# Reciprocal denominators by way of DRAM, M laid out from SBUF to SBUF, and a new order around kv, gate and up

## The chip, the cores and the metric

The kernel runs on one core of one Trainium2 chip. The metric is the device time of one execution in microseconds, the median of three runs; before the change it is 115.38 us (114.64 to 117.84). One further execution was taken with the hardware profiler: it lasted 115.02 us, of which 113.3 us are the span of its instructions.

## The reference, cut to what matters

With S = 2048 tokens of width D = 640, H = 32 heads of 20, and bf16 tensors:

```python
xn = layernorm(x)                                   # (S, D), no scale or bias
q, k, v = split(xn @ wqkv)                          # heads of 20
pq, pk = phi(q), phi(k)                             # phi(t) = t + 1 if t > 0 else exp(t), + 1e-6
kv  = einsum("hsd,hse->hde", pk, v)                 # 20 x 20 for each head
z   = pk.sum(over s)
num = einsum("hqd,hde->hqe", pq, kv)
den = einsum("hqd,hd->hq", pq, z) + 1e-6
A   = (num / den) @ wo
r   = x @ w_r                                       # B works on the same normed x
idx = the 8 tokens with the largest r
y   = (silu(x[idx] @ w_gate) * (x[idx] @ w_up)) @ w_down * sigmoid(r[idx])
B   = x, with y added to the rows idx
out = A_x + A + B
```

The attention has no softmax, so kv and wo can be folded into one 640 x 640 matrix M; then A is (pq / den) @ M, where den differs by token and head.

## The kernel before, in words

TensorE (PE) multiplies, ScalarE (ACT) and VectorE (DVE) read the products from the eight PSUM banks, SyncE (SP) issues almost all transfers, GpSimd (POOL) does the two indirect ones. The order of each engine's instructions is the order in which the Python code calls the helpers: the schedule is written by hand. Each engine's queue is served in order, so an instruction that waits holds all that stand behind it; that holds for transfers issued from ACT too. A transfer signals on one of eight semaphores, used in turn: a new transfer waits until the transfer that had its semaphore before has landed.

Up to about 61 us the kernel loops over 16 token tiles of 128: layer norm, transposed tiles xnT, k, phi(k), the Gram matrix of phi(k) and xn in PSUM (`g_mm`), and the first six of twenty query blocks. A query block is 128 features (m = 0 to 4) by 512 tokens (b = 0 to 3): `q_mm` does five products of 128x512 (L345), `q_act` two activations on ACT (exp L352, relu L353, into buffers of which there are two of each), and `q_stt` joins them on DVE into `pqT` (L357).

Then comes the tail, which the change touches. It interleaves:

- the other fourteen query blocks, `q_next(bank)`;
- den: `den_mm(b, bank)` multiplies the queries of 512 tokens by a matrix of z (20 small products, L664); `den_act` takes Ln and Exp on ACT (L671, L672), which leaves 1/den as `rden`, 128 rows (4 groups of tokens x 32 heads) by 128 tokens;
- before the change `rep_mm` (4 products with a 0/1 matrix `sel4`, L676) and `rep_ev` (ACT copy, L680) spread `rden` to `rec`, where partition p holds the reciprocals of head p // 4 for the tokens along the row; `mult` (DVE, L684) multiplies 512 tokens of `pqT` by it;
- the expert: `moe_gu_mm` (40 products, L615), `moe_silu` (three activations L621 to L623), `moe_prod` and `moe_hm` (DVE, L626, L627, L630), `moe_ht` (transpose L634, copy L635), `moe_y` (48 products with `wd`, L641, then DVE L646 and an indirect add into the DRAM copy `xd` of xn, L647), and `reload`, five transfers (L654) that read `xd` back into `xn`;
- M: `kv_mm` (30 products, L690) and `kv_ev` (DVE, L699), then for six blocks j `m_mm` (two products, L707), `m_ev` (ACT L713, DVE L714) and `m_dma(j)`. Before the change `m_dma` wrote each block to DRAM (`md`, L718) and, behind the last, read all back in five strided transfers into `m_sb` (L722), which lies as row 5p + m at partition p, block m.

Last comes the out stage: for each of 16 token tiles t ten products of 128x320 (L812) into one of three bank pairs, ACT's copy (L840), DVE's two adds in `finish` (L802 adds the reloaded xn to x for tile t + 1, L808 adds that to the copy), and a store (L809). The last tile goes by DVE alone (L850, two halves). `finish` runs a few tiles behind the products.

## Time and profile before

| | us |
|---|---|
| median of three runs | 115.38 (114.64 to 117.84) |
| profiled execution: time | 115.02 |
| profiled execution: span | 113.3 |
| PE busy | 106.1 (94%) |
| DVE busy | 87.0 (77%) |
| ACT busy | 70.2 (62%) |
| granted TensorE clock | 0.999 |

All times within an execution are counted from the start of its span. In the groups, "busy, mean ns" is the time of a group and of one instruction; "idle before" is the time for which the engine had nothing to do ahead of them, with what ended it. PE's instructions overlap, so the spacing of its products in the timeline or the chain says more than the mean of one: ten products of the out stage, one tile, stand 1.36 us apart from the next ten. In a DMA row the last figure is the time from issue to landing.

### The profile page before, as it was taken

To read this page: it belongs to the slowest core of one execution; us is meant where nothing else is said; L and a number is where in the kernel's file an instruction comes from. 1 tells how busy PE (TensorE), PEld (TensorE's weight loads), DVE (VectorE), ACT (ScalarE), POOL (GpSimd) and SP (SyncE) were. 2 spreads that over 40 slices of the span, in tenths; PEclk is the share of its full clock that TensorE was granted. 3 is DMA by queue.
4 is the path that set the end of the run, shared out by engine and by line. 5 is a ranking of instruction groups with operands and counts; after the bars stand their busy time and mean duration, and the time that the engine had idled before them with its cause. 6 is when DMAs were issued, how large, how long until landed. Compare 5 with 4: busy or idle time off the path is not lost.

```text
span 113.3 us, 2428 instructions
## 1 busy us (share of the span) xinstructions
PE 106.1 (94%) x849; PEld 66.4 (59%) x849; DVE 87.0 (77%) x217; ACT 70.2 (62%) x170; POOL 24.6 (22%) x57
## 2 busy tenths in 40 slices
PE   5998999899999989999999999999896999999970
PEld 2365655556665655556676555766453777777740
DVE  0769988999999999972266977798759449999670
ACT  4149866666866645556637779859698087655530
POOL 3022222688866233330000040000410000000000
PEclk9999999999999999999999999999999999999999
DMA  2998244799996889999996564985458998624433
GB/s 82 369 365 284 59 114 119 191 241 260 222 291 188 179 191 257 255 287 369 343 384 213 119 120 75 378 298 168 116 122 245 287 366 291 232 94 144 174 116 116
DMA packets 29389, 24.71 MB, mean 218 GB/s; under 512 B 14353, under 2 KB 28097, under 8 KB 29377
## 3 DMA queue, kind: packets, MB, share of 16 engines
q1 hardware_dynamic: 28209, 23.45, 71.8%
q10 hardware_dynamic: 992, 1.07, 2.7%
q0 software_dynamic: 176, 0.05, 0.6%
q8 instruction: 6, 0.10, 0.4%
q14 instruction: 6, 0.05, 0.1%
HBM read 15.30 MB, written 6.14 MB: 189 GB/s over the span
## 4 chain that ended last, share of the span: by engine, by line
PE 76%; ACT 8%; DVE 8%; issue 4%; POOL 1%; DVEq 0%; ACTq 0%
PE ps L812 18%; PE ps L302 14%; PE ps L345 14%; PE ps L330 13%; PE ps L231 4%; ACT rq L353 4%; DVE pk L322 2%; PE ps L332 2%; ACT eq L352 2%; PE ps L337 2%; PE ps L707 2%; PE ps L615 2%; PE ps L690 2%; DVE xn L266 1%; PE ps L273 1%
## 5 line engine op out<-in xcount | busy, mean ns | idle before, releaser
L330 PE MATMUL ps<-xn,pk 128*128 128x512 bf16 x80 | 23.5, 382 | 0.7 <-DVE pk L322 0.7
L345 PE MATMUL ps<-xnT,wq 128*128 128x512 bf16 x100 | 23.9, 381 | 0.0
L812 PE MATMUL ps<-late,pqT 128*128 128x320 bf16 x160 | 22.4, 299 | 0.9 <-ACT rq L353 0.9
L302 PE MATMUL ps<-wk,xnT 128*128 128x321 bf16 (+1 forms) x140 | 21.4, 299 | 0.6 <-ACT rq L353 0.5
L812 PEld LDWEIGHTS <-pqT 128*128 128x128 bf16 x160 | 15.5, 98 | 7.2 <-issue 1.1
L313 ACT ACTIVATE ek<-ps 128x320 bf16<-128x320 f32 x28 | 12.3, 441 | 11.9 <-PE ps L302 11.9
L302 PEld LDWEIGHTS <-xnT 128*128 128x128 bf16 x140 | 13.5, 97 | 8.4 <-ACT xnT L279 0.6
L246 POOL TENSOR_TENSOR rs<-veps,pw 128x1 f32<-128x1 bf16 x15 | 12.8, 851 | 25.8 <-DVE veps L245 25.6
L322 DVE SCALAR_TENSOR_TENSOR pk<-ek,rk 128x640 bf16<-128x640 bf16 x16 | 13.1, 819 | 5.6 <-ACT rk L314 5.5
L352 ACT ACTIVATE eq<-ps 128x512 bf16<-128x512 f32 x20 | 12.2, 608 | 8.0 <-PE ps L345 6.7
L840 ACT CAST oall<-ps 128x640 bf16<-128x640 f32 x15 | 10.2, 694 | 9.9 <-PE ps L812 9.9
L357 DVE SCALAR_TENSOR_TENSOR pqT<-eq,rq 128x512 bf16<-128x512 bf16 x20 | 13.5, 687 | 3.5 <-ACT rq L353 3.4
L345 PEld LDWEIGHTS <-wq 128*128 128x128 bf16 x100 | 10.9, 118 | 8.5 <-issue 0.3
L330 PEld LDWEIGHTS <-pk 128*128 128x128 bf16 x80 | 8.4, 117 | 7.6 <-DVE pk L322 2.6
L314 ACT ACTIVATE rk<-ps 128x320 bf16<-128x320 f32 x28 | 12.2, 436 | 0.0
L353 ACT ACTIVATE rq<-ps 128x512 bf16<-128x512 f32 x20 | 12.1, 605 | 0.0
L332 PE MATMUL ps<-xn,pk 128*128 128x129 bf16 x48 | 10.6, 220 | 0.0
L238 DVE BATCH_NORM_STATS2 st<-x_sb 128x6 f32<-128x320 bf16 x16 | 7.8, 485 | 2.3 <-DMA x_sb<-in_A_x_dram 2.3
L808 DVE TENSOR_TENSOR oall<-oall,x_sb 128x640 bf16<-128x640 bf16 x15 | 7.3, 487 | 2.5 <-ACT oall L840 2.3
L802 DVE TENSOR_TENSOR x_sb<-x_sb,xn 128x640 bf16<-128x640 bf16 x16 | 7.7, 484 | 1.5 <-DMA xn<-xd 1.5
L240 DVE BATCH_NORM_STATS2 st<-x_sb 128x6 f32<-128x320 bf16 x16 | 7.6, 476 | 0.0
L266 DVE TENSOR_SCALAR xn<-cb,rs 128x640 bf16<-128x640 bf16 x15 | 6.3, 426 | 1.6 <-POOL rs L246 1.0
(137 smaller groups left out, 115.9 us busy)
## 6 DMA issues: line engine op xcount, KB each, us to landing
xd<-xn SPq DMA_DIRECT2D x16, 160.0 KB, 3.2
x_sb<-in_A_x_dram SPq DMA_DIRECT2D x6, 320.0 KB, 4.5
wg<-in_B_w_gate_dram SPq DMA_DIRECT2D x5, 384.0 KB, 3.8
wd<-in_B_w_down_dram SPq DMA_DIRECT2D x4, 480.0 KB, 6.1
xn<-xd SPq DMA_DIRECT2D x3, 640.0 KB, 10.1
out_dram<-oall SPq DMA_DIRECT2D x12, 160.0 KB, 1.8
wu<-in_B_w_up_dram SPq DMA_DIRECT2D x3, 384.0 KB, 4.3
wq<-in_A_wqkv_dram SPq DMA_DIRECT2D x1, 800.0 KB, 6.8
```

The costliest lines, as they stand in the source:

```text
L246: pool.tensor_tensor(out=rs[:, c], in0=veps[:, c], in1=pw[:, 0:1], op=ALU.pow)
L302: pe.matmul(ps[:, KB.get((t, h), h), 0:n], lhsT=(xcT if t < 2 else xnT)[:, kc, t * P : (t + 1) * P], rhs=wk[:, kc, h * HW : h * HW + n], s ...
L313: act.activation(e[:, s], ps[:, b, 0:HW], AF.Exp, scale=c)
L314: act.activation(r[:, s], ps[:, b, 0:HW], AF.Relu, scale=c)
L322: dve.scalar_tensor_tensor(out=pk[:, t, :], in0=e[:], scalar=1.0, in1=r[:], op0=ALU.min, op1=ALU.add)
L330: pe.matmul(bank(2 + m), lhsT=w, rhs=xn[:, t, 0:512], start=(t == 0), stop=(t == T - 1))
L332: pe.matmul(ps[:, 7, m * 129 : (m + 1) * 129], lhsT=w, rhs=xn[:, t, 512 : D + 1], start=(t == 0 and m == 0), stop=(t == T - 1), skip_group ...
L345: pe.matmul(bank(bk), lhsT=wq_m[:, kc, m, :], rhs=xnT[:, kc, b * TB : (b + 1) * TB], start=(kc == 0), stop=(kc == KC - 1))
L352: act.activation(e[:], bank(bk), AF.Exp)
L353: act.activation(r[:], bank(bk), AF.Relu)
L357: dve.scalar_tensor_tensor(out=pqT[:, m, b * TB : (b + 1) * TB], in0=e[:], scalar=1.0, in1=r[:], op0=ALU.min, op1=ALU.add)
L812: pe.matmul(ps[:, bk + b, 0:HW], lhsT=pqT[:, kc, t * P : (t + 1) * P], rhs=m_sb[:, kc, b * HW : (b + 1) * HW], start=(kc == 0), stop=(kc = ...
```

## The change

1. `rep_mm` and `rep_ev` go, and `sel4` with them. Instead `rep_out` stores `rden` to a DRAM tile `rd` (32 heads x 2048 tokens; one transfer for each 512 tokens, 128 rows of 256 bytes), and `rep_in` reads it back, each head's row four times, into `rec`. For b = 0 and 1 both are issued from SP, `rep_out` between the second and third of the four loads of `wd`, `rep_in` behind `m_dma(0)`. For b = 2 and b = 3 both are issued from ACT.
2. `m_dma` is one transfer for each block, from `mt` in SBUF to `m_sb` in SBUF. `md` and the five reads go.
3. `kv_mm` and `kv_ev` stand ahead of gate and up, and one query block more stands ahead of them.
4. Banks: M takes the pairs (2,7), (3,5), (4,0), gate and up (4,0), the last five query blocks 1, 0, 6, 7, 6. `den_mm(2, 7)` stands ahead of these five blocks instead of between the fourth and the fifth.
5. The first three tiles of the out stage are no longer interleaved over the row blocks of M; each tile takes its ten products in one go.

The same on ACT's queue, where the five last query blocks stand (`eq_3`, `rq_3` are the outputs of exp and relu for b = 3; `gl` is the tile in which `rec` lies). Before:

```order
L713 CAST late<-ps 40x320
L352 ACTIVATE eq_3_1291<-ps 128x512
L353 ACTIVATE rq_3_1292<-ps 128x512
L680 CAST gl<-ps 128x512
L352 ACTIVATE eq_3_1306<-ps 128x512
L353 ACTIVATE rq_3_1307<-ps 128x512
L680 CAST gl<-ps 128x512
L352 ACTIVATE eq_3_1322<-ps 128x512
```

Changed (helpers stand some lines higher: L345 is L339 now, L352 is L346, L812 is L800, L840 is L822):

```order
L707 CAST late<-ps 40x320
L665 ACTIVATE lden<-ps,eps_111 128x128
L666 ACTIVATE rden<-lden 128x128
L670 DMA rd<-rden 4x32x128
L346 ACTIVATE eq_3_1308<-ps 128x512
L347 ACTIVATE rq_3_1309<-ps 128x512
L346 ACTIVATE eq_3_1319<-ps 128x512
L347 ACTIVATE rq_3_1320<-ps 128x512
```

The two copies from PSUM are gone from between the query blocks; den's two activations and a DMA issue stand ahead of them.

ACT's queue from the last query block into the out stage, changed (`oall` is the copy of an out tile):

```order
L347 ACTIVATE rq_3_1356<-ps 128x512
L674 DMA gl<-rd 128x1x512
L822 CAST oall<-ps 128x640 x4
L665 ACTIVATE lden<-ps,eps_111 128x128
L666 ACTIVATE rden<-lden 128x128
L670 DMA rd<-rden 4x32x128
L822 CAST oall<-ps 128x640 x2
L674 DMA gl<-rd 128x1x512
L822 CAST oall<-ps 128x640 x6
```

For b = 3 the store stands behind the copy of tile 3 and the read behind that of tile 5; the copies of tile 6 and later stand behind the read.

SP's queue from the transposes of the Gram matrix (`gp`) to the reload of `xn`, before:

```order
L508 DMA_TRANSPOSE gp<-gt 128x5x128 x5
L128 DMA wd<-in_B_w_down_dram 128x3x640 x4
L718 DMA md<-late 120x640 x5
L718 DMA md<-late 40x640
L722 DMA late<-md 128x640 x5
L654 DMA xn<-xd 128x2x640 x2
L654 DMA xn<-xd 128x4x640 x3
```

Changed (`late` holds both `mt` and `m_sb`):

```order
L502 DMA_TRANSPOSE gp<-gt 128x5x128 x5
L129 DMA wd<-in_B_w_down_dram 128x3x640 x2
L670 DMA rd<-rden 4x32x128 x2
L129 DMA wd<-in_B_w_down_dram 128x3x640 x2
L712 DMA late<-late 24x5x640
L674 DMA gl<-rd 128x1x1024
L712 DMA late<-late 24x5x640 x4
L712 DMA late<-late 8x5x640
L648 DMA xn<-xd 128x2x640 x2
L648 DMA xn<-xd 128x4x640 x3
```

Two loads of `wd` now stand behind the stores of `rd`, and the five reads of M no longer stand ahead of the reload.

```diff
--- before.py
+++ after.py
@@ -105,7 +105,8 @@
     xd = tc.dram_tile([4 * S + P, QW], BF16, name="xd")
     xd_v = xd[0 : 4 * S, :].rearrange("(t p i) d -> p t i d", p=P, i=4)
     xd_row = xd[0 : 4 * S, :].rearrange("(n i) d -> n (i d)", i=4)
-    md = tc.dram_tile([D, D], BF16, name="md")
+    rd = tc.dram_tile([H, S], BF16, name="rd")
+    rd_v = rd[:].rearrange("h (b i n) -> i h b n", b=4, i=4)
 
     ctx.enter_context(tc.manual_schedule())
 
@@ -165,13 +166,6 @@
 
     def consts_a():
         g = {}
-        one = sb([P, 4, P], BF16, "sel4")
...
-        g["sel4"] = one
         hs = sb([P, H], BF16, "hsel")
@@ -671,13 +665,13 @@
         act.activation(lden[:, b0:b1, :], ps[:, bk, c : c + n].rearrange("p (b n) -> p b n", n=P), AF.Ln, bias=eps6[:])
         act.activation(rden[:, b0:b1, :], lden[:, b0:b1, :], AF.Exp, scale=-1.0)
 
-    def rep_mm(b, bk):
-        for i in range(4):
-            pe.matmul(ps[:, bk, i * P : (i + 1) * P], lhsT=cs["sel4"][:, i, :], rhs=rden[:, b, :],
-                      start=(i == 0), stop=True, skip_group_check=True)
-
-    def rep_ev(b, bk):
-        act.copy(rec[:, b * TB : (b + 1) * TB], bank(bk))
+    def rep_out(b0, b1, q=sp):
+        for b in range(b0, b1):
+            q.dma_start(rd_v[:, :, b, :], rden[:, b, :])
+
+    def rep_in(b0, b1, q=sp):
+        n = (b1 - b0) * TB
+        q.dma_start(rec[:, b0 * TB : b1 * TB], rd[:, b0 * TB : b1 * TB].unsqueeze(1).to_broadcast([H, 4, n]))
 
     def mult(o, n):
         sl = pqT[:, :, o : o + n]
@@ -701,29 +695,28 @@
             in0=ps[0:w, bk, c0 : c0 + w].rearrange("e (m p) -> e m p", m=KC),
             in1=mkf[0:w, :, 0:n], op=ALU.mult)
 
-    def m_mm(j, bk):
+    def m_mm(j, *bk):
         w = EB if j < 5 else 40
         for b in range(2):
-            pe.matmul(ps[0:w, bk + b, 0:HW], lhsT=kvT[0:w, j, 0:w], rhs=wo[0:w, j, b * HW : (b + 1) * HW],
+            pe.matmul(ps[0:w, bk[b], 0:HW], lhsT=kvT[0:w, j, 0:w], rhs=wo[0:w, j, b * HW : (b + 1) * HW],
                       start=True, stop=True)
 
-    def m_ev(j, bk):
+    def m_ev(j, *bk):
         w = EB if j < 5 else 40
         o = mt[0:w, j, :].rearrange("p (b f) -> p b f", b=2)
-        act.copy(o[:, 0, :], ps[0:w, bk, 0:HW])
-        dve.tensor_copy(o[:, 1, :], ps[0:w, bk + 1, 0:HW])
+        act.copy(o[:, 0, :], ps[0:w, bk[0], 0:HW])
+        dve.tensor_copy(o[:, 1, :], ps[0:w, bk[1], 0:HW])
 
     def m_dma(j):
-        w = EB if j < 5 else 40
-        sp.dma_start(md[j * EB : j * EB + w, :], mt[0:w, j, :])
-        if j == NJ - 1:
-            md_v = md[:].rearrange("(p m) d -> p m d", m=KC)
-            for m in range(KC):
-                sp.dma_start(m_sb[:, m, :], md_v[:, m, :])
+        n = 24 if j < 5 else 8
+        sp.dma_start(m_sb[24 * j : 24 * j + n, :, :], mt[0 : n * KC, j, :])
+
+    def ld_wd(k0):
+        ld_w(wd, B_w_down, k0, k0 + 3)
 
     gt_stage(moe_pick)
-    for k0 in range(0, FC, 3):
-        ld_w(wd, B_w_down, k0, k0 + 3)
+    ld_wd(0)
+    ld_wd(3)
     for bk in (2, 3, 4):
         q_fin(q_next(bk))
     q1 = q_next(5)
@@ -736,63 +729,58 @@
     q_act(*q1)
     q2 = q_next(2)
     moe_xt(6)
-    den_mm(1, 7)
     q_stt(*q1[0:2])
     q_act(*q2)
-    moe_gu_mm(3, 4)
+    den_mm(1, 7)
+    q1 = q_next(3)
     q_stt(*q2[0:2])
-    moe_silu(3, 4)
     den_act(0, 2, 7)
-    moe_prod(3, 4)
+    rep_out(0, 2)
+    ld_wd(6)
+    ld_wd(9)
+    q_act(*q1)
     for j in range(4):
         kv_mm(j, 6, j * EB)
     kv_mm(4, 5, 0)
     kv_mm(5, 5, EB)
-    q1 = q_next(0)
     for j in range(4):
         kv_ev(j, 6, j * EB)
     kv_ev(4, 5, 0)
     kv_ev(5, 5, EB)
-    q_act(*q1)
-    PAIR = (2, 4, 0)
+    moe_gu_mm(4, 0)
+    moe_silu(4, 0)
+    q_stt(*q1[0:2])
+    moe_prod(4, 0)
+    moe_hm()
+    MP = ((2, 7), (3, 5), (4, 0))
     for j in range(NJ):
-        m_mm(j, PAIR[j % 3])
-        m_ev(j, PAIR[j % 3])
+        m_mm(j, *MP[j % 3])
+        m_ev(j, *MP[j % 3])
         m_dma(j)
         if j == 0:
-            moe_hm()
+            rep_in(0, 2)
         if j == 1:
-            q2 = q_next(7)
+            q1 = q_next(1)
+            q_act(*q1)
+            moe_ht(6)
+        if j == 3:
             q_stt(*q1[0:2])
             moe_gate()
-            moe_ht(6)
-        if j == 2:
-            q_act(*q2)
-        if j == 3:
-            q_stt(*q2[0:2])
         if j == 4:
             moe_y(6)
-    q1 = q_next(7)
-    q_act(*q1)
-    rep_mm(0, 6)
-    rep_ev(0, 6)
-    q2 = q_next(0)
-    q_stt(*q1[0:2])
-    q_act(*q2)
-    rep_mm(1, 7)
-    q_stt(*q2[0:2])
+    den_mm(2, 7)
+    q1 = q_next(1)
+    den_act(2, 3, 7)
+    rep_out(2, 3, act)
+    q_fin(q1)
     mult(0, 512)
-    q1 = q_next(1)
-    rep_ev(1, 7)
-    q_fin(q1)
-    q1 = q_next(6)
-    q_fin(q1)
+    q_fin(q_next(0))
     reload()
-    den_mm(2, 7)
+    q_fin(q_next(6))
+    q_fin(q_next(7))
     mult(512, 512)
-    q1 = q_next(0)
-    den_act(2, 3, 7)
-    q_fin(q1)
+    q_fin(q_next(6))
+    rep_in(2, 3, act)
     assert qn[0] == len(Q_TAIL)
 
     evac = []
@@ -813,26 +801,20 @@
                   rhs=m_sb[:, kc, b * HW : (b + 1) * HW], start=(kc == 0), stop=(kc == KC - 1))
 
     OB = (2, 4, 0)
-    for kc in range(KC):
-        for t in range(3):
-            for b in range(2):
-                out_mm(t, OB[t], kc, b)
     for t in range(T):
         bk = OB[t % 3]
         if t == 3:
-            rep_mm(2, 6)
-            rep_ev(2, 6)
             den_mm(3, 7)
         if t == 4:
             den_act(3, 4, 7)
+            rep_out(3, 4, act)
             mult(1024, 512)
         if t == 6:
-            rep_mm(3, 6)
-            rep_ev(3, 6)
+            rep_in(3, 4, act)
         if t == 8:
             mult(1536, 512)
         last = t == T - 1
-        for i in range(2 * KC if t >= 3 else 0):
+        for i in range(2 * KC):
             kc, b = (i % KC, i // KC) if last else (i // 2, i % 2)
             out_mm(t, bk, kc, b)
         if not last:
```

5 lines of the change are left out of this document (removed).

## The prediction

> **What bounds the kernel now.** I read the page first, then who waits for PE and for whom PE waits, then the chain that ended last. From the page's first part:
>
> ```profile
> PE 106.1 (94%) x849; PEld 66.4 (59%) x849; DVE 87.0 (77%) x217; ACT 70.2 (62%) x170; POOL 24.6 (22%) x57
> ```
>
> PE works 94% of the span, so a gain must be work taken from PE or a wait of PE. The waits of PE over the whole span (in all, times, longest):
>
> ```profile
> PE ps L812 <- ACT rq L353: 0.9, 1, 0.9
> PE ps L330 <- DVE pk L322: 0.7, 2, 0.4
> PE ps L676 <- DVE late L646: 0.3, 1, 0.3
> ```
>
> The first and the third lie in the tail that is changed: the out stage waits 0.9 us for the activations of the last query block, which holds bank 0, and `rep_mm` waits 0.3 us for bank 6. Together 1.2 us. The chain of the end (start, length):
>
> ```profile
> 79.10 1.22 PE ps L345 x5
> ...
> 81.43 0.48 ACT gl L680
> ...
> 87.55 3.69 PE ps L812 x26
> 91.24 0.22 PE ps L676 x4
> 91.46 0.39 PE ps L664 x20
> ...
> 96.26 12.24 PE ps L812 x90
> 108.52 0.70 ACT oall L840
> ...
> 109.66 0.48 DVE oall L850
> ```
>
> From 80.3 to 87.55 ACT sets the pace (PE runs beside it, one block ahead); from 87.55 PE alone does, at 12.24/90 = 0.136 us a product, 1.36 us a tile; behind tile 14 come its copy, an add and the last tile's two adds.
>
> **What is removed.** `rep_mm`: four calls, 0.22 us each by the row of L676: 0.88 us of PE. The two waits above: 1.2 us. So 2.1 us is what PE can gain at most here. On ACT the two copies of 0.48 us (L680) leave the stretch that it paces. The 0/1 matrix `sel4` saves POOL some work near 22 us; the most it could give PE is the later of the L330 waits, 0.33 us of that 0.7; DVE waits for ACT between the two places, so I take 0, bounds 0 to 0.33.
>
> **Kv ahead of gate and up.** The chain of before in this stretch:
>
> ```profile
> 70.39 1.75 PE ps L615 x40
> 72.14 1.74 PE ps L690 x30
> 73.88 1.21 PE ps L345 x5
> 75.09 0.62 PE ps L707 x4
> 75.71 1.08 PE ps L345 x5
> 76.80 0.17 PE ps L634 x3
> ```
>
> ACT and DVE from the timeline (start, length):
>
> ```profile
> 70.31 0.64 ACT L353 ACTIVATE rq<-ps 128x512 bf16<-128x512 f32 x1
> 72.46 0.52 ACT L623 ACTIVATE gl<-sgl 128x384 bf16<-128x384 f32 x1
> 72.85 0.56 DVE L627 TENSOR_TENSOR gl<-ps,late 128x384 bf16<-128x384 f32 x1
> 73.42 1.95 DVE L699 TENSOR_TENSOR kvT<-ps,mk 120x120 bf16<-120x120 f32 x6
> 75.81 0.35 DVE L630 TENSOR_TENSOR late<-gl 128x384 bf16<-128x384 bf16 x1
> ```
>
> PE's pieces are the same, in the order query block, kv, gate and up, M, query block, `moe_ht`. From 70.39: 1.08 gives 71.47, kv 73.21, gate and up 74.96, M 75.58, query block 76.66. DVE starts `kv_ev` when four groups of kv are there, 71.47 + 4 x 0.29 = 72.6, say 72.7, and is done at 74.7; the join of the query block (0.6, in place of 0.56 for an operation of 384 columns) 75.3, gate's and up's two reads at 0.56 (L627 and its like) 76.45, L630 76.8. `moe_ht` on PE needs that: PE arrives at 76.66 and, with the signal's way, waits 0.2. ACT's three activations of silu, 0.52 each, run from 74.2 to 75.8, in time for L630. So this move costs 0.2 us; bounds 0 (DVE a little faster) and 0.5.
>
> SP waits here for `rden`: den's activations follow ACT's block at 70.95 and take about 0.9 (two of the width of L623), so `rep_out` issues at 71.9, and the two last loads of `wd`, which stood right behind the first two, come at about 72.8 and 73.3. `moe_y` needs the last quarter near 78.7 (it lies between 76.80 and 79.10 before). The transfers (KB, us from issue to landing; then L718, M's writes to DRAM, with the issue's length in ns and the landing, and the landing of L722, M's reads):
>
> ```profile
> wd<-in_B_w_down_dram SPq DMA_DIRECT2D x4, 480.0 KB, 6.1
> xd<-xn SPq DMA_DIRECT2D x16, 160.0 KB, 3.2
> out_dram<-oall SPq DMA_DIRECT2D x12, 160.0 KB, 1.8
> xn<-xd SPq DMA_DIRECT2D x2, 320.0 KB, 5.3
> L718 SPq DMA_DIRECT2D md<-late x6: 278/326/1134, 76.6 to 81.2; - x6
> DMA to landing us min/median/max: 2.0/2.8/2.9
> DMA to landing us min/median/max: 2.3/3.0/3.7
> ```
>
> The last load at 73.3 + 6.1 would be 79.4, 0.7 too late; but 6.1 holds four loads in a row behind transposes, and now half of the bytes are through when these two start. I take 0, bounds 0 and 0.7.
>
> **M.** One transfer a block, priced at L718's 2.8, at most 2.9: the last issues near 81, as before (81.2) and lands near 83.9; the out stage, which now needs all blocks for its first product, starts after 85. The five reads were not waited for either. Nothing; bounds 0 and 0.5. The reload stands behind five issues fewer and comes about 1 us earlier; that frees DVE earlier, not PE.
>
> **The five last query blocks.** `moe_ht` to the first of them took 2.3 us on PE (76.80 to 79.10); from 76.85 that is 79.15, and `den_mm(2)`, 0.39, ends at 79.55. ACT then has den's two activations and the store:
>
> ```profile
> 85.57 0.43 ACT L671 ACTIVATE lden<-ps,eps 128x128 f32<-128x128 f32 x1
> 86.03 0.31 ACT L672 ACTIVATE rden<-lden 128x128 bf16<-128x128 f32 x1
> 104.51 0.36 ACTq L809 DMA_DIRECT2D out_dram<-oall  x1
> ```
>
> 0.1 for the signal, 0.77 and 0.36 end at 80.8, when PE's first block (79.55 + 1.08 = 80.65) is there. Then 1.1 us a block: 81.9, 83.0, 84.1; the fourth waits for a buffer that DVE frees behind `mult(0)` and a join, about 84.9 to 86.0; the fifth 87.1. PE waits about 0.1 for bank 0 (DVE's last M half) at the second block, and 0.1 to 0.2 for bank 6 at the fifth (84.15 for 84.0); then it goes straight into tile 0, whose banks 2 and 3 are long free. New waits in all 0.2 + 0.2 = 0.4. If the issue held ACT for as much as 1.1 (the longest of L718), PE would lose 0.8 more; bounds 0 and 0.8.
>
> **The out stage.** Sum: 0.88 + 1.2 - 0.4 = 1.7 us earlier. Tile 14 ends at 108.5 - 1.7 = 106.8, tile 3 at 91.84, tile 5 at 94.56. ACT's copy of tile 3 (0.70) and den's activations (0.7, overlapping a little) end 1.36 later, 93.2; there `rep_out(3)` issues. ACT is through with tile 5 at 95.25 and then stands at `rep_in(3)` until the store has landed; PE feels that only when tile 9 needs a bank at 98.64. What depends on the landing of `rep_in(3)` is DVE:
>
> ```profile
> 97.77 1.48 DVE L684 TENSOR_TENSOR pqT<-pqT,gl 128x2560 bf16<-128x2560 bf16 x1
> 99.17 0.48 DVE L802 TENSOR_TENSOR x_sb<-x_sb,xn 128x640 bf16<-128x640 bf16 x1
> 99.57 0.48 DVE L808 TENSOR_TENSOR oall<-oall,x_sb 128x640 bf16<-128x640 bf16 x1
> ```
>
> Behind `mult(1536)` stand ten pairs of adds (tiles 5 to 14) at 0.80 (0.40 from one start to the next). If the read lands at L, DVE has tile 14 at L + 1.48 + 8.0. Undelayed it has it at 106.8 + 0.70 + 0.45 = 107.95. So the trip is free up to L = 98.45, 5.2 us after 93.2. Bounds for it: the store 1.8 (`out_dram`, wide rows) to 3.2 (`xd`, rows of 320 bytes), the read 2.3 to 3.7 (L722's shortest and longest): 4.1 to 6.9. These small transfers run with few others behind them (the reload began earlier), so I stand nearer to the short end, 4.6: free. At 6.9 it costs 1.7. The Trainium skill (DMA: Bandwidth & Descriptors, Specifications) has a rule against this change: runs below 512 bytes make the DMA engine read, modify and write. The 3.2 of `xd` beside the 1.8 of `out_dram`, for equal bytes, agrees in sign, though `xd` runs under more traffic; by the rule the store's price is the 3.2, and with a read of 2.3 the trip is 5.5 and costs 0.3. For b = 2 the read, issued behind the fifth block at 87.1, lands before 93.2 even at 5.3 us, and PE wants `mult(1024)` at tile 8, 97.3; for b = 0 and 1 several us are spare.
>
> **The rivals.** *The trip sits on the end (A).* It lasts 5.2 to 7.0 us; DVE ends late by the excess. For it: two transfers in series, medians 2.8 and 3.0, 5.8, cost 0.6. Gain 0 to 1.7, about 1.0: 114.4. *The trip blocks (B), slower.* `rep_out(3)` and `rep_in(3)` take what the reload's transfers take, 5.3 each, 10.6: L = 103.8, tile 14 at 113.3 instead of 107.95, 5.3 lost for 1.7 won: 119.0. The point where it turns slower than before is 6.9 us, slower by 2% near 9.2. Against it: the reload's 5.3 is of 320 KB, and the small ones go through ACT's queue. *ACT stays the bound (C).* The store's issue and the two-buffer ring hold the query blocks: gain 0.9, 114.5; likewise if `wd` is late. *Hardly any new wait (D).* The 0.4 does not appear, POOL's 0.33 does: gain 2.4, 113.0. That the M path changes nothing is in the sum already.
>
> **The numbers.** Against the profiled execution: 115.02 - 1.7 = 113.3. The median of the runs lies 0.36 above that execution, so 113.7. Chances: this forecast (113.1 to 114.1) 0.46; A 0.20; B 0.08; C 0.12; D 0.14. A measurement of this kernel tells some 2% (2.3 us, 113.07) from no change. Faster by over 2%: D, and the forecast's lower edge with the scatter of medians, 0.14 + 0.08 = 0.22. Slower by over 2%: the half of B beyond 9.2 us and other mishaps, 0.06. Within: 0.72. The range goes from D, with 0.3 for scatter, 112.7, to the far end of A, 115.2; it leaves out B and a little of D and C.
>
> **What would show it.** Right: no L676 on PE; PE's wait for L353 ahead of the out stage gone; a wait of 0.2 at `moe_ht`; 22.2 us from the out stage's first product to its last; DVE's `mult(1536)` starting at or below 98.5 and DVE waiting for ACT's copies again at the end. Wrong: DVE waiting for a DMA ahead of `mult(1536)` to 99 or later with L808 back to back up to the end (A, B); PE waiting at L641 for `wd`, or for ACT among the last query blocks by more than 0.4 (C).

## Result, and the profile after

The changed kernel takes 114.6 us (median of 13 executions, 113.27 to 119.12) where the kernel before, beside it on the same chip, takes 114.85 (13 executions, 114.64 to 117.84). The ratio is 0.9938, with a 95% interval of 0.9913 to 0.9963: about 0.7 us less, a gain of 0.6%, far inside the 2% that count as no change. The ratios leave out executions more than 1.5% above the fastest of their kernel, and the changed kernel scatters more widely than that, so the median and range of all executions stand beside each ratio; by the medians it is 0.25 us less. A second set of twelve executions of the same file gave 114.87 (113.84 to 116.55) beside 114.76, ratio 0.9981 [0.9945, 1.0016]. So the change is worth something between nothing and 1 us, where 1.7 had been worked out.

The first profiled execution of the changed kernel took 119.12 us and lost 2.0 us near its start, waiting for a load of `wk`. The lines of after below are therefore from a second profile of the unchanged file, an execution of 113.92 us; where the first one is meant, the text says so. Helpers stand at the lines that the order rows on the change give (L339 is the query block, L800 the out stage, L822 its copy, L678 `mult`).

The page's first line and its busy times:

```profile
span 112.2 us, 2399 instructions
PE 104.7 (93%) x833; PEld 65.1 (58%) x833; DVE 85.8 (76%) x217; ACT 68.4 (61%) x166; POOL 23.1 (21%) x54
```

PE has 1.4 us less work than before (106.1). Its waits (in all, times, longest; the first two lie in the part that changed, the third in the loop over token tiles):

```profile
PE ps L635 <- DMA wd<-in_B_w_down_dram: 0.7, 1, 0.7
PE ps L339 <- ACT rq L347: 0.6, 1, 0.6
PE ps L324 <- DVE pk L316: 0.3, 1, 0.3
```

The waits for bank 6 at L676 and for bank 0 ahead of the out stage are gone. Two others have come, for the last load of `wd` at `moe_y` and for ACT among the last query blocks, 1.3 together where 0.4 had been charged. PE's timeline (start, length) from the query blocks to the out stage:

```profile
79.53 0.46 PE L658 MATMUL ps<-pqT,zm 128*32 128x128 bf16 x20
79.92 4.51 PE L339 MATMUL ps<-xnT,wq 128*128 128x512 bf16 x20
85.03 1.24 PE L339 MATMUL ps<-xnT,wq 128*128 128x512 bf16 x5 [0.60 <-ACT rq L347]
86.21 4.24 PE L800 MATMUL ps<-late,pqT 128*128 128x320 bf16 x30
```

Den's products start at 79.53, where the prediction had them at 79.15, though this execution had come into the tail 0.6 us earlier than the one before; of the 1.0 us so lost the wait for `wd` is 0.7. The out stage starts at 86.21. Before, it started effectively at 87.01 (87.55, less four products of 0.136 us that had run ahead).

DVE in the out stage, and the chain of the end (start, length):

```profile
94.57 1.49 DVE L678 TENSOR_TENSOR pqT<-pqT,gl 128x2560 bf16<-128x2560 bf16 x1 [3.71 <-DMA gl<-rd]
108.67 0.88 DVE L832 TENSOR_TENSOR oall<-ps,x_sb 128x320 bf16<-128x320 f32 x2
```

```profile
80.78 1.11 ACTq L670
...
86.86 7.69 DMA gl<-rd
...
95.98 0.48 DVE x_sb L790
...
109.15 0.40 DVE oall L832
```

The read for b = 2, issued at 86.86, lands 7.69 us later. DVE stands for 3.71 us in front of `mult(1024)`, and from there on adds back to back until the last tile. The chain of the end no longer runs through PE alone but through ACT's store issue, the read of `rd` and DVE.

Two stretches sum up all profiles. The first goes from `den_mm(0)` to the first product of the out stage, the second from there to the end of the last add. In every kernel where nothing holds it, the second lasts 23.53 us with the products for b = 2 and b = 3 in it, so 23.31 with one of them and 23.09 without the two (0.22 each; worked out, no kernel reached the 23.09), and "lost" is what lies above that. Times in us, from PE's and DVE's timelines, one execution each; gaps of 0.2 us that the profile puts down to nothing ("issue") are left out. The named kernels follow below. Four of these executions are long ones for their kernel: the first profile of after (119.12 us, median 114.6), mult10 (115.44, median 114.05), Monly (115.40, median 114.56) and b23pe_md (115.48, the longest of twelve).

| kernel | den_mm(0) at | to the out stage | out stage to end | lost there | what PE waited for in the first stretch |
|---|---|---|---|---|---|
| before | 67.03 | 19.98 | 23.53 | 0 | ACT 0.9, DVE 0.3 |
| after, first profile | 69.52 | 20.06 | 25.18 | 2.1 | ACT 0.9, `wd` 0.3, DVE 0.3 |
| same | 66.41 | 19.80 | 23.34 | 0.25 | `wd` 0.7, ACT 0.6 |
| mult10 | 66.34 | 20.48 | 24.26 | 1.2 | M 1.3, ACT 0.6 |
| b3pe | 66.83 | 19.96 | 23.44 | 0.1 | ACT 0.8, `wd` 0.4, DVE 0.2 |
| wdfirst | 66.41 | 19.28 | 25.09 | 2.0 | ACT 0.5, M 0.3 |
| b23pe | 66.80 | 20.56 | 23.53 | 0 | M 1.9 |
| Monly | 67.58 | 19.97 | 23.53 | 0 | ACT 0.9, DVE 0.3 |
| b23pe_md | 66.81 | 19.84 | 24.52 | 1.0 | M 0.8 (and 0.7 behind it), `wd` 0.4 |
| pool_wd | 66.66 | 19.63 | 23.49 | 0.4 | M 1.1 |
| poolspread | 66.63 | 19.37 | 24.14 | 1.05 | M 0.8 |
| spread | 66.83 | 19.32 | 23.53 | 0 | M 0.8 |
| mearly | 67.04 | 19.02 | 23.53 | 0 | DVE 0.7 |
| noM | 67.00 | 18.38 | 23.53 | 0 | nothing |

The prediction's walk through the stretch, which put the fifth query block at 84.15 and so the out stage at about 85.35, makes 18.3 us of the first column of lengths (85.35 - 67.03). `same` took 19.80.

### The profile page after: what moved, and what is told of

It reads as the page before. It is cut to its first block, busy times and chain, and to the rows that moved or that the text cites. A ratio compares the mean times of both kernels' runs of the same rounds, so it can differ in the third digit from the quotient of the medians.

```text
span 117.4 us, 2389 instructions
## 1 busy us (share of the span) xinstructions
PE 105.4 (90%) x823; PEld 65.8 (56%) x833; DVE 86.0 (73%) x217; ACT 68.4 (58%) x166; POOL 23.1 (20%) x54
## 4 chain that ended last, share of the span: by engine, by line
PE 37%; DVE 24%; DMA 17%; issue 8%; ACT 7%; POOL 2%; SPq 2%; ACTq 1%; DVEq 1%
PE ps L296 11%; PE ps L339 8%; PE ps L324 6%; DMA wk<-in_A_wqkv_dram 6%; PE ps L800 5%; DMA wd<-in_B_w_down_dram 5%; DVE x_sb L790 4%; DMA rd<-rden 4%; DVE pk L316 3%; DVE st L234 3%; DVE st L232 3%; DVE xn L260 3%; ACT rq L347 2%; DMA gl<-rd 2%; DVE pqT L351 2%
## 5 line engine op out<-in xcount | busy, mean ns | idle before, releaser
L339 PE MATMUL ps<-xnT,wq 128*128 128x512 bf16 x96 | 22.7, 380 | 1.4 <-ACT rq L347 0.9
L800 PE MATMUL ps<-late,pqT 128*128 128x320 bf16 x160 | 22.2, 299 | 0.9 <-ACT oall L822 0.5
L324 PE MATMUL ps<-xn,pk 128*128 128x512 bf16 x74 | 22.0, 381 | 0.4 <-DVE pk L316 0.2
L800 PEld LDWEIGHTS <-pqT 128*128 128x128 bf16 x160 | 15.5, 98 | 7.5 <-DVE pqT L351 0.8
L346 ACT ACTIVATE eq<-ps 128x512 bf16<-128x512 f32 x20 | 12.1, 606 | 8.3 <-PE ps L339 5.0
L822 ACT CAST oall<-ps 128x640 bf16<-128x640 f32 x15 | 10.1, 694 | 11.6 <-PE ps L800 5.1
L339 PEld LDWEIGHTS <-wq 128*128 128x128 bf16 x100 | 11.1, 118 | 9.9 <-issue 1.2
L678 DVE TENSOR_TENSOR pqT<-pqT,gl 128x2560 bf16<-128x2560 bf16 x4 | 6.0, 1490 | 5.8 <-DMA gl<-rd 5.8
```

The lines of the kernel that those rows point to most:

```text
L324: pe.matmul(bank(2 + m), lhsT=w, rhs=xn[:, t, 0:512], start=(t == 0), stop=(t == T - 1))
L339: pe.matmul(bank(bk), lhsT=wq_m[:, kc, m, :], rhs=xnT[:, kc, b * TB : (b + 1) * TB], start=(kc == 0), stop=(kc == KC - 1))
L346: act.activation(e[:], bank(bk), AF.Exp)
L800: pe.matmul(ps[:, bk + b, 0:HW], lhsT=pqT[:, kc, t * P : (t + 1) * P], rhs=m_sb[:, kc, b * HW : (b + 1) * HW], start=(kc == 0), stop=(kc = ...
```

## The experiments

Two theories were set against each other. The first, called T1 in the expectations, is that the trip of the reciprocals over DRAM sits on the end (the prediction's rival A). The other, theory M, is that M's six transfers, which the prediction priced at nothing, hold the out stage back. The wait for `wd` (theory W) and that for ACT's store issue (T2, later A) are tested beside them; T3 is that other small waits come back whatever the transfers do. "After" and "before" in the diffs name the file that is edited.

**The same kernel again (same).** No edit.

> The changed kernel as it is, for an execution whose start is not disturbed. Theory T1 (the trip of the last reciprocals, b = 3, over DRAM ends late and DVE's ten pairs of adds trail behind it up to the end): DVE waits 1 to 3 us for the read of rd ahead of its last multiplication, its adds then stand back to back to the last tile, and PE's last product is done over 0.5 us before DVE reaches the last tile. Theory T2 (the store of b = 2, issued from ACT, holds ACT over 1 us and the last query blocks with it): an issue over 1 us on ACT near 81 us and a wait of PE of about 0.9 us ahead of the fifth of the last query blocks. Theory T3 (the work taken from PE comes back as other small waits ahead of the out stage, whatever the transfers do): neither. Time against before by the runs so far: 0.994.

Measured: 114.87 (12 executions, 113.84 to 116.55) beside 114.76, ratio 0.9981 [0.9945, 1.0016]. The profile is the one shown above. T2's two signs are there, the issue over 1 us on ACT and the wait at the fifth block (0.6 us). T1's wait is there too, but for the read of b = 2. In the first profile that read held DVE as well (2.5 us), but it was b = 3's trip that set the end. There the chain of the end reads:

```profile
97.05 4.59 DMA rd<-rden
101.66 2.64 DMA gl<-rd
...
105.80 0.48 DVE x_sb L790
```

It took 7.3 us from the issue of the store to the landing of the read, DVE waited 3.34 us in front of `mult(1536)`, and its adds ran back to back to the end. In `same` the trip of b = 3 took 4.8 us (93.68 to 98.48) and nothing waited for it. So in both executions the end hung on a transfer of `rd`, but on a different one, at a cost of 2.1 us in one and of 0.25 in the other.

**Ask for the reciprocals of b = 3 two tiles later (mult10).**

```diff
--- after
-        if t == 8:
+        if t == 10:
             mult(1536, 512)
```

> The changed kernel, but the last multiplication of DVE (tokens 1536 on) stands two tiles later in the program, ahead of tile 10 instead of tile 8. The transfers are the same; DVE can do some three pairs of adds (2.4 us) in the time in which it waited. T1: DVE's wait for the read falls by up to 2.4 us, the end comes 0.7 to 1.3 us earlier than in the changed kernel, against before 0.983 to 0.988. T2 and T3: within 0.3 us of the changed kernel, 0.991 to 0.997; if PE now waits for the multiplication at tile 12, slower.

Measured: 114.05 (7 executions, 113.53 to 118.34) beside 114.76, ratio 0.9913 [0.9881, 0.9945]. That is T2's and T3's range; T1's 0.983 to 0.988 was missed. Its profile is of a long execution, 115.44 us, and shows what can still hold the kernel when the trip has 2.7 us more. PE's waits:

```profile
PE ps L800 <- DMA late<-late: 1.3, 1, 1.3
PE ps L800 <- ACT oall L822: 1.0, 1, 1.0
PE ps L339 <- ACT rq L347: 0.6, 1, 0.6
```

and ACT's queue in the out stage:

```profile
94.90 1.45 ACT L822 CAST oall<-ps 128x640 bf16<-128x640 f32 x2 [0.65 <-PE ps L800]
99.39 0.55 ACTq L674 DMA_DIRECT2D gl<-rd  x1
99.98 1.88 ACT L822 CAST oall<-ps 128x640 bf16<-128x640 f32 x3 [3.63 <-PE ps L800]
```

The store, issued at 94.28, had landed only at about 99.4, 5.1 us later, and until then ACT stood at the read with the copies of the next tiles behind it; PE ran out of banks for 1.0 us. That is the way to the bound that the prediction's out-stage part described and took for harmless. And the out stage itself started late, at 86.82: PE waited 1.3 us for a transfer of M (`late<-late`).

**b = 3 by products again (b3pe).**

```diff
--- after (sel4, rep_mm and rep_ev as before)
-            rep_out(3, 4, act)
             mult(1024, 512)
         if t == 6:
-            rep_in(3, 4, act)
+            rep_mm(3, 6)
+            rep_ev(3, 6)
```

> The changed kernel with the reciprocals of b = 3 spread by four products and an ACT copy, as before the change; b = 0, 1 and 2 still go over DRAM. T1: the trip of the end is gone, for 0.22 us more on PE: 0.5 to 1.1 us faster than the changed kernel, 0.984 to 0.990 of before. T2: as the changed kernel or 0.2 us slower, 0.994 to 0.997. T3: the same as T2.

Measured: 114.2 (8 executions, 113.68 to 114.74), ratio 0.9951 [0.9924, 0.9978].

```profile
PE ps L346 <- ACT rq L354: 0.8, 1, 0.8
PE ps L642 <- DMA wd<-in_B_w_down_dram: 0.4, 1, 0.4
```

The out stage loses only 0.1 us now, and the scatter of its 8 executions, 1.1 us, is less than half that of the 12 of `same`. The first stretch is no shorter (19.96), since `wd` and ACT hold PE there. T1 may explain a part of the changed kernel's scatter, but not the missing gain: the ratio lies in the range of T2 and T3, and as the only cause T1 falls.

**b = 2 and b = 3 by products (b23pe).** The same edit for both, at tiles 3 and 6; ACT issues no transfer of `rd` any more.

```diff
--- after (sel4, rep_mm and rep_ev as before)
     den_act(2, 3, 7)
-    rep_out(2, 3, act)
...
-    rep_in(2, 3, act)
...
         if t == 3:
+            rep_mm(2, 6)
+            rep_ev(2, 6)
             den_mm(3, 7)
```

> The changed kernel with the reciprocals of b = 2 and b = 3 spread by products, as before; ACT issues no store and no read. T1 without T2: as the kernel with b = 3 alone by products, 0.1 to 0.3 us slower than that for the 0.22 us of PE. T2: faster than that one by 0.5 to 1.0 us, since the issue of over 1 us is gone from between ACT's query blocks: near 0.980 of before if T1 holds too, near 0.986 if only T2 does. T3: 0.994 to 0.998, PE's products come back and nothing else changes.

Measured: 115.32 (12 executions, 113.87 to 115.72), ratio 1.0011 [0.9977, 1.0045]. The waits for ACT and `wd` are gone, and the one that was behind them comes into view:

```profile
PE ps L813 <- DMA late<-late: 1.9, 1, 1.9
L727 SPq DMA_DIRECT2D late<-late x6: 698/812/2146, 77.0 to 83.7; - x6
```

The second row is SP's issue of M's six transfers (length in ns, shortest, median and longest; first and last start). One takes SP 0.81 us, and up to 2.15. The last starts at 83.7, and the transfer that PE waits for lands at 87.0. The ratio is above every forecast, T3's too. Taking the trip of b = 2 and 3 away gained nothing: M takes its place.

**M's six transfers left out (noM).** b23pe without them; the out stage multiplies by five blocks of `wd`, which are there long before, in place of M, so its output is another one. M's products and their copies are still made.

```diff
--- b23pe
         m_ev(j, *MP[j % 3])
-        m_dma(j)
...
-                  rhs=m_sb[:, kc, b * HW : (b + 1) * HW], start=(kc == 0), stop=(kc == KC - 1))
+                  rhs=wd[:, kc, b * HW : (b + 1) * HW], start=(kc == 0), stop=(kc == KC - 1))
```

> The kernel with the reciprocals of b = 2 and 3 by products, without the six transfers of M: the out stage multiplies by five blocks of wd, which lie in SBUF since long, in M's place (the products of M and their copies are still made). Theory M (the landing of M sets the start of the out stage): the wait of 1.9 us goes, PE starts the out stage near 85.5 us, and the kernel is 1.2 to 1.9 us faster than the one with the transfers (1.001 of before): 0.984 to 0.991, with a scatter as small as that of before. If PE is held by something else at that place as well (ACT, wd, the reciprocals): 0.995 to 1.001.

Measured: 113.97 (11 executions, 113.01 to 116.98; ten of them up to 114.78) beside 114.76, ratio 0.9918 [0.9899, 0.9938], so 1.35 us below b23pe by the medians.

```profile
79.87 5.67 PE L346 MATMUL ps<-xnT,wq 128*128 128x512 bf16 x24 [0.18 <-issue]
85.38 4.24 PE L812 MATMUL ps<-wd,pqT 128*128 128x320 bf16 x30
```

The out stage starts at 85.38 with no wait ahead of it. The prediction's walk gave about 85.35, and its steps before that fit too: kv starts at 71.41 (walk 71.47), gate and up at 73.11 (73.21), `moe_ht` at 76.82 (76.85). So the walk was right where no transfer held PE. This shows M's transfers to be what b23pe waits for.

**M straight to its place, everything else as before (Monly).**

```diff
--- before
-        sp.dma_start(md[j * EB : j * EB + w, :], mt[0:w, j, :])
...
+        n = 24 if j < 5 else 8
+        sp.dma_start(m_sb[24 * j : 24 * j + n, :, :], mt[0 : n * KC, j, :])
```

> The kernel before the change with one part alone: M goes from SBUF to SBUF in six transfers; reciprocals by products, order, banks and out stage as before. Theory M: the issues cost SP 0.8 us each here too; the last block lands near 85 to 86 us where PE of before starts its out stage at 85.9, so PE waits 0 to 0.5 us for M and for ACT as before: 0.998 to 1.004. Theory W and A: the M path is neutral or frees the reload, 0.997 to 1.001, and PE waits for ACT only.

Measured: 114.56 (12 executions, 114.36 to 115.47) beside 114.70, ratio 0.9996 [0.9979, 1.0013].

```profile
88.09 2.20 PE L807 MATMUL ps<-late,pqT 128*128 128x320 bf16 x15 [0.91 <-ACT rq L352]
```

As before, the out stage waits 0.9 us for ACT, and M is there by then: its last share landed at 85.40. The new path of M does no harm while ACT is later. Only a kernel that gets rid of ACT's wait meets it.

**M over DRAM in the new order (b23pe_md).** b23pe with `md`, the five reads and the old interleaving of the first three tiles.

```diff
--- b23pe
-        sp.dma_start(m_sb[24 * j : 24 * j + n, :, :], mt[0 : n * KC, j, :])
+        sp.dma_start(md[j * EB : j * EB + w, :], mt[0:w, j, :])
+        if j == NJ - 1:
+            md_v = md[:].rearrange("(p m) d -> p m d", m=KC)
+            for m in range(KC):
+                sp.dma_start(m_sb[:, m, :], md_v[:, m, :])
```

> The changed kernel with the reciprocals of b = 2 and 3 by products and with M over DRAM in its old order (the out stage's first three tiles interleaved again). What is left of the change: b = 0 and 1 over DRAM, kv ahead of gate and up, the banks. Theory M: the kernel with M from SBUF to SBUF waited 1.9 us for M; this one starts the out stage near 85.9 us and is 1.0 to 1.5 us faster than it, 0.987 to 0.993 of before. If M was not the cause (W or A): 0.998 to 1.003, as that one.

Measured: 114.79 (12 executions, 114.38 to 115.48), ratio 0.9994 [0.9972, 1.0016].

```profile
PE ps L818 <- DMA late<-md: 1.4, 3, 0.8
```

The time is what was forecast for the case that M is not the cause. But over DRAM, too, PE waits for M, 1.4 us in three pieces, and 0.4 us for `wd`, in this one execution, the longest of the twelve. So, as far as it shows, it is not that one way of M is bad and the other good: once ACT no longer holds PE, PE is too early for either.

**`wd` ahead of the stores of `rd` (wdfirst).**

```diff
--- after
     ld_wd(3)
+    ld_wd(6)
+    ld_wd(9)
...
     rep_out(0, 2)
-    ld_wd(6)
-    ld_wd(9)
```

> The changed kernel with all four loads of wd issued right behind the transposes, as before the change; the two stores of rd follow them. Theory W (the wait of moe_y for wd, 0.3 to 0.7 us in three of five traced executions, is a part of the missing gain): no wait for wd on PE, 0.3 to 0.6 us faster than the changed kernel, 0.990 to 0.995 of before. Theory M (the six transfers of M, issued at 0.8 us each instead of 0.33, land at 86 to 87 us and set the start of the out stage): PE comes to the out stage earlier and waits there for M instead, 0.995 to 1.000. Theory A (ACT: the store of b = 2 and the reads that it stands at): the same as M in time, but PE's wait is for ACT.

Measured: 115.34 (6 executions: 113.23, 113.78, 115.13, 115.54, 116.17, 116.32) beside 114.70. The ratio, 0.9893 [0.987, 0.9916], holds only two of the six; the medians' is 1.0055. On the time this run is inconclusive. On the wait it isn't: none for `wd`, and the out stage starts earlier, with the next cause in front of it.

```profile
85.69 1.52 PE L800 MATMUL ps<-late,pqT 128*128 128x320 bf16 x10 [0.30 <-DMA late<-late]
DVE pqT L678 <- DMA gl<-rd: 5.7, 2, 3.1
```

The first stretch is 0.5 us shorter than in `same`, and the out stage 1.75 longer: DVE waits twice for a read of `rd`, 5.7 us in all. The trip of b = 3 took 7.2 us here and 4.8 in `same`, most of it in the store (4.45 for 2.08). This execution took 115.13 us, the third shortest of the six.

**All of it on another queue (pool_wd).** After with `wd` first, `mult(1536)` at tile 10, and the stores and reads of b = 2 and 3 issued by POOL instead of ACT.

```diff
--- after (wd as in wdfirst, t == 10 as in mult10)
-    rep_out(2, 3, act)
+    rep_out(2, 3, pool)
...
-    rep_in(2, 3, act)
+    rep_in(2, 3, pool)
...
-            rep_out(3, 4, act)
+            rep_out(3, 4, pool)
...
-            rep_in(3, 4, act)
+            rep_in(3, 4, pool)
```

> The changed kernel with wd loaded first, the last multiplication ahead of tile 10, and the stores and reads of b = 2 and b = 3 issued from POOL, which has nothing else to do then; M as in the change. Theory A: ACT holds no transfer, so PE's waits for ACT ahead of the out stage and in it go: 0.982 to 0.988 of before. Theory M: PE is at the out stage near 85.4 us and waits for M until 86.5 to 87: 0.990 to 0.995. If POOL's transfers are slow (its indirect ones take 1.3 to 1.6 us to issue and 3.2 to land, a trip of 8 to 9 us), DVE waits for the read at the end and it is no faster than the changed kernel.

Measured: 114.81 (12 executions, 113.43 to 118.12), ratio 0.9976 [0.9947, 1.0005].

```profile
86.29 4.24 PE L800 MATMUL ps<-late,pqT 128*128 128x320 bf16 x30 [1.08 <-DMA late<-late]
DVE pqT L678 <- DMA gl<-rd: 5.2, 2, 4.0
```

Ahead of the out stage PE waits neither for ACT nor for `wd` any more, and 1.08 us for M: the wait has moved to the next that was late. The reads still come 5.2 us late for DVE, but `mult(1536)` two tiles later leaves only 0.4 us of that at the end.

**M's transfers over two queues (spread, poolspread).** On b23pe with `wd` first, and on pool_wd: blocks 1 and 3 are issued by POOL, and so is the first read of `rd`, which stood between M's transfers on SP.

```diff
--- b23pe (wd as in wdfirst) / pool_wd
-        sp.dma_start(m_sb[24 * j : 24 * j + n, :, :], mt[0 : n * KC, j, :])
+        (pool if j in (1, 3) else sp).dma_start(m_sb[24 * j : 24 * j + n, :, :], mt[0 : n * KC, j, :])
...
     rep_out(0, 2)
+    rep_in(0, 2, pool)
...
         if j == 0:
-            rep_in(0, 2)
+            pass
```

> Reciprocals of b = 2 and 3 by products, wd loaded first, the read of rd for b = 0 and 1 on POOL as soon as it is stored, and blocks 1 and 3 of M issued from POOL too, so that SP has four issues of 0.8 us instead of six and the read. Theory M: the last block lands about 1.5 to 2 us earlier, PE waits 0 to 0.5 us for M: 0.986 to 0.992 of before. If the landing of M is set by the DMA engines and not by the issues: the wait stays at 1 to 2 us, 0.997 to 1.002.

> The kernel with the transfers of b = 2 and 3 on POOL, wd first and the late last multiplication, with M spread in the same way over SP and POOL. Theory M: its wait of 1.1 us for M goes to 0 to 0.4: 0.984 to 0.991 of before; against the kernel with products for b = 2 and 3 it saves 0.44 us of PE and may lose it to DVE's wait for the reads at the end. If the DMA engines set the landing: 0.995 to 1.000.

Measured: spread 113.97 (6 executions, 113.45 to 114.22), ratio 0.9922 [0.9901, 0.9943]; poolspread 114.28 (7 executions, 113.5 to 114.77), ratio 0.9944 [0.9914, 0.9974]. The rows of spread, PE's timeline, POOL's issues and the chain:

```profile
86.15 1.11 PE L814 MATMUL ps<-late,pqT 128*128 128x320 bf16 x7 [0.78 <-DMA late<-late]
L727 POOL DMA_DIRECT2D late<-late x2: 641/666/692, 78.2 to 79.1; - x2
L727 SPq DMA_DIRECT2D late<-late x4: 697/782/867, 77.1 to 80.6; - x4
79.11 6.34 DMA late<-late
```

SP is through with M 3 us earlier (its last issue starts at 80.6 instead of 83.7), and PE's wait falls from 1.9 to 0.8. That lies between the two forecasts, since M lands only 1.1 us earlier. The chain names a transfer of POOL's, issued at 79.11 and landed at 85.45, but it only infers who ended a wait. PE's queue stood until 85.99, and the block that SP issued at 79.52 landed at 85.95, 6.43 us later: this one is what is left. Issuing earlier bought little, because the blocks then took longer to land (in b23pe the one that PE waits for took 4.20 us). poolspread differs from spread in keeping the trip, and pays for it:

```profile
PE ps L801 <- DMA late<-late: 0.8, 1, 0.8
PE ps L801 <- ACT oall L823: 0.8, 1, 0.8
```

With nearly the same start of the out stage, it loses 1.05 us behind it where spread loses nothing. PE waits for ACT's copy, the copy 2.0 us for DVE, and DVE had waited 3.4 us for the read of b = 3.

**M earlier (mearly).** spread, with the first two of M's blocks ahead of the join of gate and up and the last two ahead of `moe_y`; `den_mm(2)` goes behind the first two of the last five query blocks, `moe_gate` ahead of kv, and the banks follow.

```diff
--- spread
-    MP = ((2, 7), (3, 5), (4, 0))
...
+    MP = ((2, 7), (3, 4))
...
+    m_all(0)
+    m_all(1)
+    moe_prod(0, 1)
+    moe_hm()
+    q2 = q_next(5)
+    m_all(2)
+    m_all(3)
+    moe_ht(6)
+    q_stt(*q1[0:2])
+    m_all(4)
+    m_all(5)
+    q_act(*q2)
+    q3 = q_next(0)
+    moe_y(6)
```

> The kernel with M spread over SP and POOL and with the products for b = 2 and 3, reordered so that the six blocks of M are copied from PSUM before the sigmoid's and gate's work and before two more query blocks: the last block's transfer issues near 79.5 us instead of 81. Transfers and their queues are the same. Theory M (M's landing alone is left of what holds PE there): PE waits 0 to 0.3 us for M instead of 0.8, the out stage starts near 85 us instead of 86.15: 0.982 to 0.988 of before, 0.4 to 1.1 us faster than that kernel (0.992). If one slow DMA engine decides when M lands, whenever it is issued: the wait is as long as before, 0.991 to 0.997. If the reordering costs PE a new wait (for DVE ahead of the transposes or of moe_y): 0.990 to 0.996.

Measured: 113.67 (6 executions, 113.57 to 114.18) beside 114.80, ratio 0.9909 [0.9891, 0.9927]. This is the best of all versions, 0.9% below before and by the medians 0.9 us below the changed kernel, and has the least scatter; its interval overlaps spread's.

```profile
77.92 0.34 PE L635 MATMUL ps<-ident,late 128*128 128x128 bf16 x3 [0.66 <-DVE late L631]
82.69 3.43 PE L346 MATMUL ps<-xnT,wq 128*128 128x512 bf16 x15
86.06 1.11 PE L820 MATMUL ps<-late,pqT 128*128 128x320 bf16 x7
L727 SPq DMA_DIRECT2D late<-late x4: 698/782/867, 76.1 to 80.9; - x4
```

The wait for M is gone from PE, but M is not earlier. SP's last issue, forecast near 79.5, starts at 80.9 (spread: 80.6), and the last block lands at 85.87 (spread: 85.95), 0.19 us before PE's first product of the out stage. PE meets it later instead: 0.66 us at `moe_ht`, where DVE is now late, is the price of the new order, about what separates it from noM's 18.38 in the first stretch (19.02). That is the third case of the forecast, a new wait for DVE, and the ratio lies in its range. Whether M can land earlier by being issued earlier is not tried by this run.

## Why the prediction was right, and where it wasn't

The time fell inside the range (112.7 to 115.2) and into "within 2%", which had 0.72. It did so on a forecast, 113.7, whose reasons held in one half. Its gain of 1.7 us came to 0.7 in the first set and 0.2 in the second. The range held because it took in A and C: the 114.6 lies nearest to these rivals, not to the forecast, and beside a before of 114.85 the forecast's gain would have given 113.2. Of the prediction's own signs of being wrong, PE's waits for `wd` and for ACT among the last query blocks came in both profiles, and DVE's wait for a transfer ahead of `mult(1536)` came in the first.

**PE's part held.** `rep_mm` took 0.88 us of PE, and PE's out stage, from its first product to the end of its last, lasts 22.40 us in `same` where spread's lasts 22.84, 0.44 shorter; the waits for bank 6 and bank 0 went. The walk of PE, ACT and DVE through kv, gate and up and the five query blocks put the out stage at about 85.35, and noM starts it at 85.38. The shifts that this part charged for, 0.2 at `moe_ht` and bank 0, are not to be seen as waits in `same`.

**The step that failed by most is "M. One transfer a block, priced at L718's 2.8 ... Nothing; bounds 0 and 0.5".** It took over the landing time of the old writes, and their issue times with it. L718's own row in the prediction has a median issue of 0.33 us. The new transfer, three-dimensional and from SBUF to SBUF, takes 0.70 at least and 0.81 in the median, so six of them some 5 us of SP's time instead of 2. SP's last issue starts at 82.2 to 83.7 instead of 81.2. The landing was off as well: a block took 2.9 to 6.8 us from the start of its issue, over all profiles that have this path, where 2.8 had been set. The chains of wdfirst, pool_wd, mult10 and b23pe have the transfer that PE waits for landing at 85.55, 86.05, 86.57 and 87.01 instead of 83.9. PE waits 0.3 to 1.9 us for it in wdfirst, mult10, b23pe, pool_wd, spread and poolspread, that is, up to four times the upper bound. In `same` this wait doesn't show, since PE is late enough by the other two; but there, too, the last block landed at 86.08, 0.13 us before PE's first product of the out stage, and in all ten profiles with this path in the new order that margin is 0.13 to 0.35. By this, PE would have stood there for M if ACT's wait alone had gone. The sentence behind it, that the reads hadn't been waited for either, was true of a PE that waited for ACT until 87.55, and the change removes just that wait.

**Three terms were set at the wrong end of their bounds, and one of them left its bounds.** The wait for `wd` behind the stores of `rd` was taken as 0, with bounds 0 and 0.7; it is 0.3 (first profile), 0.4 (b3pe, b23pe_md) and 0.7 (same), and goes when `wd` stands first. The store's issue on ACT was taken as 0.36 from the out stores; it is 1.11 in `same` and 1.40 in the first profile:

```profile
80.78 1.11 ACTq L670 DMA_DIRECT2D rd<-rden  x1
93.68 0.58 ACTq L670 DMA_DIRECT2D rd<-rden  x1
```

The second row is the same store for b = 3, when SP isn't issuing M: the longest value named in the prediction (1.1) was about right for b = 2, and the 0.8 us that it said PE would lose is the 0.5 to 0.9 that PE waits for ACT at the fifth block; b23pe and pool_wd, without that issue on ACT, have no such wait. The trip of b = 3 was taken as 4.6 us, bounds 4.1 to 6.9, free up to 5.2. From the start of the store's issue to the landing of the read it took 4.8 in `same`, as set, but 7.2 to 8.4 in the five other profiles that have it (7.25 in the first, 7.7 in mult10, 7.2 in wdfirst, 7.7 in pool_wd, 8.4 in poolspread), above the upper bound. It is the store that was under-priced: it took 2.08 in `same` and 4.45 to 5.52 in the five, where the read took 2.55 to 2.86 in all six. The read of b = 2, thought safe "even at 5.3", was the one that came late in `same`. The reason given for the short end, that few other transfers run beside it, was argued and never shown; what was left unweighed for b = 2 is that the reload of `xn` (2.6 MB) is issued on SP from 84.15 on, just ahead of the read at 86.86. Amid the reload that read took 4.5 to 8.0 us in the seven profiles that have it; the read for b = 3, behind the reload, took 2.55 to 2.86 in six. The Trainium skill's rule in the prediction (DMA: Bandwidth & Descriptors, Specifications), read-modify-write below 512 bytes, would have the store slow: in the first profile that of b = 3, with its 256-byte runs, landed after 4.59 us, later than even the 3.2 that the rule picked. But the runs show another condition. The store of b = 0, with the same runs, landed after 2.2 to 2.8 us in the seven profiles where the last two loads of `wd` stand behind it, and after 4.8 to 5.3 in the five where they stand ahead of it; wdfirst (5.23) differs from `same` (2.24) in this order alone. That the rule has a share in this isn't shown by any run.

**One term had a gain after all.** `sel4` off POOL was taken as 0, bounds 0 to 0.33. Five profiles without it wait for `pk` once, 0.3 us (the row shown above), where six of the seven with it and no late `wk` wait twice, 0.7, as before; b23pe, which waits once and has its `den_mm(0)` no earlier, is the exception. Their `den_mm(0)` stands at 66.49 on average for 66.91 (before, b3pe, b23pe, b23pe_md, noM, spread, mearly), 0.4 earlier. About 0.2 of that is the second wait that is gone (PE stands 1.64 us from one product to the next there, for 1.86 before); the rest arises in the first 11 us and may be scatter.

**By rivals:** A (114.4) and C (114.5) both came to pass in part: the out stage loses 0.25 to 2.1 us in all five kernels that kept the trip for b = 3, and PE waits for ACT among the query blocks in three of these. B's condition, a trip of more than 6.9 us, came true in five of six profiles, but its result, slower than before, only in single executions. D didn't happen. The sum for `same` closes: 0.6 us earlier into the tail, 0.18 gained in the first stretch instead of 1.66 by the walk, 0.19 in the out stage instead of 0.44, 1.0 in all, and its last add ends at 109.55 for 110.54.

What the other transfers in flight explain of the landings is shown above for the store and the read of `rd`; how much of M's landing they explain stays open. A transfer's shares are counted as they land. In b23pe, one of M's transfers has 11 of its 12 by 84.94 and the last at 86.82, and the one that PE waits for has 11 by 86.25 and the last at 87.01; in mult10 it is 83.11 and 85.57, and 85.60 and 86.57. So one share of the twelve comes 0.8 to 2.5 us behind the others. In b23pe a packet of 16 KB of the queue named "instruction", 1.98 us long, ends at 82.3. Such packets are suspected, but every profile has one near there, the one of before too (1.29 us from 79.36), and no run here takes them away.

## What to carry to other kernels

When a wait is removed from the critical engine, reprice every transfer that ended inside the old wait, with the issue time of its new shape as well as its landing: here four things (M, `wd`, ACT's store, the trip) stood within 1 to 2 us behind the wait that went, and each could take back a part. A few products that replicate a small row on a nearly full PE (0.22 us for four) can still be cheaper than a free-looking trip over DRAM, if that trip's slowest execution, not its typical one, reaches the end. Issuing transfers earlier from two queues need not make them land as much earlier: in spread 3 us at the last issue became 1.1 us at the landing. And a wait that vanishes has not always been removed: in mearly PE came later, and M landed when it had before.

## What the runs showed of the hardware

The time that a queue takes to issue a DMA differed with the transfer and with the moment. On SP a write of 120 rows of 640 to DRAM took 0.33 us in the median (0.41 in b23pe_md), a transfer of 24x5x640 from SBUF to SBUF 0.81; shape and destination differ here together. On ACT the same store of 4x32x128 took 0.58 later on and 1.11 to 1.40 while SP was issuing M, in all five profiles. SP's longest issue of M in `same`, 1.75 us from 80.17, lies beside that store (80.78 to 81.89) and beside POOL's indirect transfer (80.06 to 81.67). But b23pe's longest, 2.15 us from 80.57, has only POOL's transfer beside it, and one of mult10, 0.77 us from 80.10, has both. Whether the queues stretch each other wasn't tried by itself and stays open.

A transfer of 150 KB or less took up to 7 or 8 us to land (a block of M 6.80 in spread, a read of `rd` 7.99 in b3pe), counted from the start of its issue, where the prediction had looked at 2.8 for the median. The same transfer took up to three times as long with others in flight: the 32-KB store of b = 0 took 4.8 to 5.3 us behind all loads of `wd` and 2.2 to 2.8 with two of them behind it, the read of 128 KB 4.5 to 8.0 amid the reload and 2.55 to 2.86 behind it. It lands with the last of its shares: M's transfers, 24 rows of one side and 120 of the other, counted 12 shares and the stores of `rd`, 4x32x128, counted 4, each behind one earlier update. The Trainium skill (DMA: Bandwidth & Descriptors, section "Why a DMA increments its semaphore by 16 and not by 1") gives the rule, the largest number up to 16 that divides the slowest dimensions of both sides, by which these two give 12 and 4; the trace agrees.

The scatter differed between versions. Six executions each of mearly and spread, which end on PE, span 0.6 and 0.8 us; twelve of the changed kernel, with the trip, span 2.7 in the second set. That the trip is the reason isn't shown: noM, which ends on PE too, has one execution in eleven at 116.98, and before some up to 117.84.
